# All engine orders of a fused attention and snake MLP kernel planned anew, with later assumed landings for units 4 to 11

## The chip, the core and the metric

One core of a Trainium2 chip. The metric is the time of one execution in microseconds on the device; lower is better.

## The reference

Two layers, one after the other, in float32 (the kernel works in bf16 with float32 sums):

```python
# linear attention with decay, blocks of 64 positions; B, H, S, D = 4, 8, 768, 64
for b in range(S // 64):
    qb, kb, vb = q[:, :, sl], k[:, :, sl], v[:, :, sl]
    intra = einsum('bhij,bhjd->bhid', einsum('bhic,bhjc->bhij', qb, kb) * Dmask, vb)
    inter = einsum('bhid,bhde->bhie', qb * lam_pow, kv_state)
    out[:, :, sl] = intra + inter
    kv_state = lam_block * kv_state + einsum('bhsd,bhse->bhde', kb * rev_pow, vb)
# snake MLP on x = out as 3072 tokens x 512
h = x @ w_in                     # 512 x 2048
g = h + sin(alpha * h) ** 2 / (alpha + 1e-9)
y = g @ w_out                    # 2048 x 512
```

## The kernel before

The attention is cut into 12 units (u = 0 to 11) of one batch and 256 positions, all eight heads. The MLP is cut into 6 chunks of 512 tokens; chunk c takes the outputs of units 2c and 2c+1.

For one unit the steps are:
- Loads of k, q and v (512 KB each) on SyncE's queue (`load_unit`, line 385 issues them), into one of three float32 buffers.
- Preparation, `uscale`: k is cast to bf16 (line 509), q and v are multiplied by powers of lam (line 523). There are two halves of heads of each, so six operations, each given to POOL, VectorE (DVE) or, for k, ScalarE (ACT). The result is `qkv`, a ring of three units.
- Transposes of q and k into `qkT`. Units 0 to 3 do it on TensorE (`upiece_T`, line 539, with a copy in line 548); units 4 to 11 do it by two DMA transposes on SyncE's queue (`upiece_D`, line 555).
- Matmuls in small tiles (line 578): scores, state sums and outputs (`urun` for the first units, `upair` for units 4 to 11, where one piece holds the scores and sums of unit u with the outputs of unit u-1). VectorE masks the scores (`Smu`, lines 658 and 767) and keeps the states (`Zs`, lines 671 and 778); ScalarE or POOL casts the states (`Zu`, lines 674 and 781); the outputs go to `xT` (lines 688 and 788).

For a chunk, an "a" unit is h for 128 of the 2048 columns and all 512 tokens (`unit_A`, four matmuls, line 811); an "h" unit is 256 columns and half of the tokens (`unit_A2`, eight matmuls, line 845). ScalarE takes the sine (t, lines 821 and 855), POOL or ScalarE the square (u, lines 825, 826, 859 and 860), VectorE joins them (gT, lines 828 and 863). A "b" unit is four of the 16 matmuls that give one 128 x 512 tile of the result (`unit_B`, line 876); after the fourth, ScalarE copies it out (line 890) and stores it.

The order of the work is set by a planner that runs when the kernel is built (`_Plan`). Every operation is given with an assumed duration; a DMA also with an assumed latency `lat` behind its transfer. The planner starts, one after the other, the operation that can begin first by these assumptions. SyncE keeps the order in which the program gives its operations (for each unit u: its transposes, then the loads of unit u+2). TensorE may take any of its next 40. ScalarE, VectorE and POOL take whatever is ready by the assumed times. Nothing of this is decided at run time: each engine then executes its fixed order, and waits at an operation whose inputs are not there.

Two lists written out by hand steer it. `HEAD` gives the loads and steps of units 0 and 1, with an engine and a bank behind the colon: `lk01` loads half 1 of unit 0's k, `q00:POOL` prepares half 0 of unit 0's q on POOL, `Tq01:2ACT` transposes by bank 2 with the copy on ACT, `S`, `O` and `Z` are scores, outputs and sums, `W` casts a staged part of w_in, `D` and `E` are loads of w_in and w_out in POOL's queue, with the load that they wait for behind the colon, and `F` is the order of free PSUM banks. `ORDER` is TensorE's list from there on: `a`, `h` and `b` units (chunk, then numbers), `g` for the next attention piece (18 in all; the tenth begins unit 4, the eleventh unit 5, and so on) and `s`, which leaves out one PSUM bank in the rotation of free banks. Matmuls of constants (`spin`, line 947) fill TensorE's idle time in the first 26 us of the plan.

Of the kernel before, what the change touches and what calls it, by code (L numbers as in the profile page):

```python
# [35 lines left out]
class _Plan:  # L36
# [21 lines left out]
    def op(self, eng, emit, dur, reads=(), writes=(), dma=None, after=(), issue=0.4, lat=2.6, runs=64):  # L58
        o = _Op(eng, emit, dur, tuple(reads), tuple(writes), dma, after, issue, lat, runs)
        for b in o.reads:  # L60
            if b in self.writer:
                o.deps.add(self.writer[b])
        for b in o.writes:
            if b in self.writer:
                o.deps.add(self.writer[b])
            o.deps.update(self.readers.get(b, ()))
        o.deps.update(after)
        for b in o.reads:
            self.readers.setdefault(b, []).append(o)
        for b in o.writes:  # L70
            self.writer[b] = o
            self.readers[b] = []
        o.deps.discard(o)
        o.lead = self.lead
        self.ops.append(o)
        return o
# [211 lines left out]
def bass_lightning_attn__then__act_snake_kernel(  # L288
# [34 lines left out]
    with es:  # L323

        def sb(name, shape, dt):
            return es.enter_context(nc.sbuf_tensor(name, shape, dt))
# [19 lines left out]
        qkT = sb("qkT", [128, RT, 8, 128], BF16)  # L346
# [25 lines left out]
        def _(_unused_eng):  # L372
# [4 lines left out]
            op = P.op  # L377
# [6 lines left out]
            def load(dst, src, key, dur, sem, eng="SP", lat=2.6, after=(), issue=0.4, runs=64):  # L384
                return op(eng, lambda e: e.dma_start(dst, src), dur, dma=sem, lat=lat, after=after, issue=issue, runs=runs,  # L385
                          writes=key if isinstance(key, list) else [key])

            def at(u):

                return 2 * (u // NB) + u % 2, u % NB // 2  # L390

            def load_unit(u, which, g=None, after=()):
                (b, n), j = at(u), u % (RL // 2)
                for nm in which:
                    src = {"q": q, "k": k, "v": v}[nm]
                    hs = slice(0, H) if g is None else slice(4 * g, 4 * g + 4)
                    if nm == "q":
                        dst = q32[j][:, hs, :, :].rearrange("p h t d -> p h (t d)")
                        keys = [("q32", j, i) for i in range(2) if g in (None, i)]
                    else:  # L400
                        dst = (k32 if nm == "k" else v32)[j][:, :].rearrange("p (h x) -> p h x", x=2 * D)[:, hs, :]
                        keys = [(nm + "32", 2 * j + i) for i in range(2) if g in (None, i)]
                    last[nm, u] = last[nm, u, g] = load(
                        dst, src[b, hs, 2 * BL * n:2 * BL * (n + 1), :].rearrange("h (p t) d -> p h (t d)", t=2),
                        keys, 1.82 if g is None else 0.91, f"u{nm}{j}" + ("" if g is None else str(g)),
                        lat=2.7 if g is None else 2.9, after=after, runs=64 if g is None else 32,
                    )

            def load_w1(i, after):
# [17 lines left out]
            def load_w2(i, after):  # L427
# [6 lines left out]
            last = {}  # L434
            load(lam_bc[:, :], bass.AP(lam.tensor, 0, [[0, 128], [1, H]]), "lam", 0.1, "lam", "ACT", runs=1)
            load(alphaT[:, :], bass.AP(moe_alpha.tensor, 0, [[128, NM], [1, 128]]), "alphaT", 0.1, "alphaT", "ACT", lat=4.9, runs=1)
            HEAD = """lk01 lv00 lq00 lk00 lv01 F:1564073 lq01 lq10 q00:POOL lk10 q01:POOL lk11 k11:ACT lq11 Tq01:2ACT lv10
                lv11 k10:POOL Tq00:1ACT q10:POOL v01:DVE k01:POOL D1:v11 k00:POOL Tk00:0ACT lw256 q11:DVE Tk01:7DVE
                S0:0 Tk1:2ACT lw0 D2:w0 v00:DVE Z0:6 S1:0 X0 O0:5 v10:POOL v11:POOL W256:ACT Z1:4 Tq1:0ACT O1:6 X1
                S2:6 S3:0 D3:v11 O3:0 E0:q11 W0:DVE A0.2:7 E1:w0 O2:4 A0.0:6""".split()  # L440
            for item in HEAD:
                if item[0] == "l":
                    if item[1] == "w":
                        load_w1_first(int(item[2:]))
                    else:
                        load_unit(int(item[2]), item[1], int(item[3]))
# [47 lines left out]
            def reg_keys(u, which, g):  # L494
                return [("u" + which, u % 3, g)]
# [5 lines left out]
            def uT_key(u, which, g):  # L501
                return ("qT" if g == 0 else "kT", 2 * (u % 3) + (which == "k"))
# [49 lines left out]
            def upiece_D(u, which):  # L552
                sl, i = 2 * (u % 3) + (which == "k"), 0 if which == "q" else 1024
                flat = qkv[:, 2 * (u % 3):2 * (u % 3) + 2, :, :].rearrange("p a b c -> p (a b c)")[:, i:i + 1024]
                op("SP", lambda e: e.dma_start_transpose(qkT[:, sl, :, :], flat), 1.0,  # L555
                   [x for g in range(2) for x in reg_keys(u, which, g)], [uT_key(u, which, g) for g in range(2)],
                   dma=f"qkT{sl}", runs=16, lat=2.1, issue=1.3)

            made = {}

# [308 lines left out]
            def unit_B(c, s4, mq, ob, lo=0, hi=DM, out_eng="ACT"):  # L869
# [26 lines left out]
                    return store  # L896
                store(out_eng)

            ORDER = """h0.1.2 h0.1.0 h0.1.12 h0.1.4 b0.0.0 h0.1.6 b0.2.0 h0.0.14 h0.0.4 a0.9 h0.0.12 g b0.1.0 h0.1.14
                h0.0.6 a0.8 s s b0.1.1 s s a0.10 g a0.11 s g s b0.2.1 b0.0.1 b0.1.2 b0.2.2 g b0.1.3 g b0.0.2 s  # L900
                b0.0.3 s s s g g g g h1.0.6 h1.0.0 b0.3.0 s b0.3.1 b0.2.3 h1.0.12 a1.9 s b0.3.2 s s b0.3.3 g a1.2
                a1.3 h1.1.6 a1.8 h1.1.0 a1.4 b1.0.0 a1.5 a1.11 a1.10 a1.14 a1.15 b1.0.1 h1.1.12 s b1.0.2 g s b1.0.3
                g b1.1.0 b1.1.1 b1.2.0 h2.0.4 b1.1.2 h2.0.10 a2.0 a2.7 b1.2.1 a2.1 a2.2 a2.6 s b1.1.3 b1.2.2 h2.1.4
                b1.3.0 b1.2.3 s a2.3 s g s s s b1.3.1 h2.1.10 b1.3.2 b1.3.3 s h2.0.14 h2.0.12 b2.0.0 a2.8 a2.9
                b2.1.0 s h2.1.14 h3.0.8 s s b2.0.1 h3.0.4 s b2.1.1 s b2.1.2 b2.0.2 s s s s b2.0.3 s g h2.1.12 s s
                a3.7 h3.0.0 h3.1.0 s s b2.2.0 b2.2.1 b2.1.3 b2.3.0 a3.14 h3.0.2 a3.6 h3.1.4 b2.2.2 a3.15 b2.3.1
                b2.2.3 s g s b2.3.2 s a3.12 s b2.3.3 s b3.0.0 b3.1.0 s h3.0.10 a3.13 h3.1.2 s b3.0.1 s s s s b3.0.2
                b3.0.3 b3.1.1 s s h3.1.8 s b3.1.2 g s a4.8 s h3.1.10 b3.1.3 b3.3.0 s b3.2.0 a4.1 s b3.2.1 a4.6
                b3.2.2 b3.2.3 s g s a4.2 a4.9 b3.3.1 a4.3 a4.0 s s b3.3.2 g s s b4.1.0 a4.5 a4.15 a4.10 a5.4 s s s
                a4.7 b3.3.3 s a4.13 a4.4 s b4.3.0 s b4.0.0 s a5.6 s s s s s a5.3 a5.12 a5.11 b4.3.1 b4.0.1 b4.2.0  # L910
                a5.8 s a4.11 a5.7 a5.13 s b4.1.1 a5.9 b4.1.2 s s a5.15 s a5.0 a5.2 b4.0.2 a5.5 a5.1 b4.2.1 a4.14 s
                a4.12 b5.2.0 s b4.2.2 a5.10 s s s b5.3.0 s b4.3.2 b4.0.3 b5.1.0 s s b5.3.1 b5.1.1 s a5.14 b5.1.2
                b5.0.0 b5.1.3 s b4.2.3 b5.0.1 b5.0.2 b5.0.3 b5.2.1 b4.3.3 b4.1.3 b5.3.2 b5.2.2 s b5.2.3 b5.3.3"""
            late = {}
            for item in HEAD:
                name, _, what = item.partition(":")
                kind = name[0]
                u, g = int(name[1]) if name[1:2].isdigit() else None, int(name[-1]) if name[-1].isdigit() else None
                if kind in "kqv":
                    uscale(u, kind, g, what)  # L920
                elif kind == "T":
                    u, gs = int(name[2]), [int(x) for x in name[3:]] or [0, 1]
# [35 lines left out]
            for u in range(2, U0):  # L958
                s = 2 * u
# [11 lines left out]
            for u in range(U0, NU + 1):  # L971
                if u < UD:
                    pieces += [([4], lambda u=u: upiece_T(u, "k", [0, 1], 4)), ([5], lambda u=u: upiece_T(u, "q", [0, 1], 5))]
                pieces.append(([1, 2, 3, 4, 5, 6, 7], lambda u=u: upair(
                    u if u < NU else None, u - 1 if u > U0 else None)))
                outs_at[u - 1] = len(pieces) if u > U0 else outs_at[u - 1]
            ahead = [(0, lambda: load_unit(2, "kqv", None, [last["w1", 3]])), (0, lambda: load_w2(3, [last["k", 2]])),
                     (0, lambda: load_unit(3, "kqv"))]
            for u in range(2, NU):
                ahead.append((outs_at[u - 3] if u > 4 else 0, lambda u=u: uprep(u)))  # L980
                for which in "kq" if u >= UD else "":
                    ahead.append((0, lambda u=u, which=which: upiece_D(u, which)))
                if u + 2 < NU:
                    ahead.append((0, lambda u=u: load_unit(u + 2, "kqv")))
            done, todo = 0, ORDER.split()
            for i, token in enumerate(todo):
# [71 lines left out]
```

## Time and profile before

| what | value |
| --- | --- |
| median of 3 runs | 219.35 us (218.84 to 219.45) |
| the profiled execution | 219.23 us, span 217.5 us |
| granted TensorE clock | 1.00 |
| TensorE, matmuls | 202.1 us busy, 93% of the span |
| ScalarE | 145.0 us busy, 67% |
| VectorE | 130.8 us busy, 60% |
| POOL | 98.3 us busy, 45% |
| moved by DMA | 34.45 MB |

Busy time counts an engine's instructions; "idle before" and the bracket at the end of a timeline row give the engine's idle time just before an instruction and what ended it. PE is TensorE, SPq is SyncE's DMA queue. A row of stretches holds the length, then for each engine the busy time and in brackets the instructions, then granted clock, DMA share and GB/s. A row of waits holds the sum in us, the number of waits and the longest.

### The profile page before, as it was taken

The numbers are of one execution on the slowest core, as the hardware profiler recorded it, in microseconds if no ns is written. First come the engines' busy times: TensorE is split into PE (matmuls) and PEld (weight loads), VectorE is DVE, ScalarE is ACT, GpSimd is POOL, SyncE is SP. The second block draws the span as 40 slices with busy tenths as digits, with TensorE's granted clock in tenths as the row PEclk, the third lists the DMA queues.
The fourth block names the chain that finished last, engine by engine and source line by source line (L and its number), as shares of the span: only waits on it lengthen the run. The fifth ranks groups of instructions, "written<-read, shape, count | busy, mean of one in ns | idle before, by whom it ended". The sixth has DMA issues, their size and how long they took to land.

```text
span 217.5 us, 5371 instructions
## 1 busy us (share of the span) xinstructions
PE 202.1 (93%) x2251; PEld 113.3 (52%) x2274; DVE 130.8 (60%) x214; ACT 145.0 (67%) x263; POOL 98.3 (45%) x110
## 2 busy tenths in 40 slices
PE   4899999799989897999699999999999999999995
PEld 1355775364645455555465655556454444444454
DVE  2676668788889964754683674844457555652100
ACT  2586789453769735786585885864869688794431
POOL 2577768364577965751972751510006231310000
PEclk9999999999999999999999999999999999999999
DMA  4999999999999999999993911502011000001242
GB/s 111 300 311 227 207 267 268 242 276 323 274 236 271 292 214 301 228 222 285 189 294 102 127 24 56 92 2 99 3 48 51 0 0 0 3 2 62 79 150 99
DMA packets 62985, 34.45 MB, mean 158 GB/s; under 512 B 18272, under 2 KB 60016, under 8 KB 62960
## 3 DMA queue, kind: packets, MB, share of 16 engines
q1 hardware_dynamic: 55632, 24.25, 50.0%
q0 software_dynamic: 3696, 3.67, 10.2%
q10 hardware_dynamic: 3632, 6.17, 8.3%
q8 instruction: 18, 0.29, 0.6%
q14 instruction: 7, 0.06, 0.1%
HBM read 27.28 MB, written 6.29 MB: 154 GB/s over the span
## 4 chain that ended last, share of the span: by engine, by line
PE 57%; DMA 22%; POOL 6%; SPq 5%; DVE 4%; issue 2%; ACT 2%; ACTq 0%
PE bank L876 28%; PE bank L811 16%; DMA q<-in_q_dram 9%; PE bank L845 7%; DMA v<-in_v_dram 6%; PE bank L578 6%; DMA w<-in_moe_w_in_dram 4%; SPq L385 4%; POOL qkv L523 3%; DMA k<-in_k_dram 2%; POOL u L826 2%; DVE Smu L767 1%; SPq L555 1%; DVE gT L828 1%; DVE qkv L523 1%
## 5 line engine op out<-in xcount | busy, mean ns | idle before, releaser
L876 PE MATMUL bank<-w,gT 128*128 128x512 bf16 (+1 forms) x383 | 88.0, 370 | 3.1 <-issue 1.4
L828 DVE SCALAR_TENSOR_TENSOR gT<-u,rinv,bank 128x512 bf16<-128x512 bf16 x60 | 43.5, 744 | 27.1 <-ACT u L825 17.0
L876 PEld LDWEIGHTS bank<-w,gT 128*128 128x128 bf16 x400 | 38.0, 98 | 41.5 <-DVE gT L828 1.7
L811 PE MATMUL bank<-xT,w 128*128 128x512 bf16 x234 | 56.1, 379 | 0.5 <-issue 0.2
L821 ACT ACTIVATE t<-bank,alpha 128x512 bf16<-128x512 f32 x60 | 39.9, 686 | 13.1 <-PE bank L811 12.2
L863 DVE SCALAR_TENSOR_TENSOR gT<-u,rinv,bank 128x256 bf16<-128x256 bf16 x72 | 31.2, 475 | 13.6 <-POOL u L860 9.8
L845 PE MATMUL bank<-xT,w 128*128 128x256 bf16 x288 | 35.5, 273 | 1.9 <-DVE Smu L767 1.8
L811 PEld LDWEIGHTS bank<-xT,w 128*128 128x128 bf16 x240 | 22.9, 98 | 27.1 <-ACT xT L788 1.1
L855 ACT ACTIVATE t<-bank,alpha 128x256 bf16<-128x256 f32 x72 | 30.4, 472 | 9.7 <-PE bank L845 9.1
L845 PEld LDWEIGHTS bank<-xT,w 128*128 128x128 bf16 x288 | 27.5, 98 | 10.1 <-DVE Smu L767 2.7
L826 POOL TENSOR_TENSOR u<-t 128x512 bf16<-128x512 bf16 x21 | 21.7, 1039 | 22.5 <-ACT t L821 15.1
L860 POOL TENSOR_TENSOR u<-t 128x512 bf16<-128x512 bf16 x23 | 24.0, 1057 | 11.4 <-ACT t L855 11.4
L890 ACT COPY osb<-bank 128x512 f32<-128x512 f32 (+1 forms) x25 | 14.2, 568 | 18.9 <-PE bank L876 18.9
L767 DVE TENSOR_TENSOR Smu<-bank,masku 128x1024 bf16<-128x1024 f32 x16 | 19.0, 1219 | 11.0 <-PE bank L578 11.0
L825 ACT ACTIVATE u<-t 128x512 bf16<-128x512 bf16 x39 | 24.4, 629 | 1.0
L523 POOL TENSOR_TENSOR qkv<-q,Lq 128x512 bf16<-128x512 f32 x15 | 17.5, 1177 | 15.9 <-DMA q<-in_q_dram 15.9
L523 POOL TENSOR_TENSOR qkv<-v,Lv 128x512 bf16<-128x512 f32 x16 | 18.0, 1134 | 13.2 <-PE bank L578 9.3
L788 ACT CAST xT<-bank 128x512 bf16<-128x512 f32 x15 | 10.5, 741 | 7.6 <-PE bank L578 7.6
L947 PE MATMUL bank<-masku,ident 128*128 128x512 bf16 x33 | 10.8, 435 | 2.7 <-DVE masku L461 2.7
L523 DVE TENSOR_TENSOR qkv<-q,Lq 128x512 bf16<-128x512 f32 x9 | 7.4, 821 | 7.4 <-DMA q<-in_q_dram 7.4
L509 POOL CAST qkv<-k 128x512 bf16<-128x512 f32 x12 | 7.3, 611 | 8.5 <-DMA k<-in_k_dram 8.5
L658 DVE TENSOR_TENSOR Smu<-bank,masku 128x1024 bf16<-128x1024 f32 x8 | 9.7, 1218 | 2.2 <-PE bank L578 2.2
(56 smaller groups left out, 139.8 us busy)
## 6 DMA issues: line engine op xcount, KB each, us to landing
out_dram<-osb ACTq DMA_DIRECT2D x23, 256.0 KB, 2.4
k<-in_k_dram SPq DMA_DIRECT2D x10, 512.0 KB, 5.4
q<-in_q_dram SPq DMA_DIRECT2D x10, 512.0 KB, 7.2
v<-in_v_dram SPq DMA_DIRECT2D x10, 512.0 KB, 8.0
w<-in_moe_w_out_dram POOLq DMA_DIRECT2D x4, 512.0 KB, 8.7
w<-in_moe_w_in_dram POOLq DMA_DIRECT2D x3, 512.0 KB, 9.3
k<-in_k_dram SPq DMA_DIRECT2D x4, 256.0 KB, 5.5
v<-in_v_dram SPq DMA_DIRECT2D x4, 256.0 KB, 5.3
```

Of the source, the lines that this page charges most:

```text
L523: emit = lambda e: e.tensor_tensor(dst, src, tab, ALU.mult)
L767: op("DVE", lambda e, g=g: e.tensor_tensor(Smu[(2 * S + g) % 4][:, :, :, :, :].rearrange("p a b c i -> p (a b) (c i)"), bass.AP(banks, 512 ...
L811: ins = e.matmul(ps[hb][:, c0:c1], w1[:, kc, 128 * m:128 * (m + 1)], xT[x][:, kc, c0:c1], start=(kc == 0 and c0 == lo), stop=(kc == NKC - ...
L821: op("ACT", lambda e: e.activation(t16[ju][:, w], ps[hb][:, w], ACTF.Sin, scale=alpha[:, m:m + 1]), 0.69 * f, [bank(hb), "alpha"], [("t16" ...
L825: lambda e: (e.activation(u16[ju][:, w], t16[ju][:, w], ACTF.Square) if e is nc.scalar else e.tensor_tensor(u16[ju][:, w], t16[ju][:, w], ...
L826: e.tensor_tensor(u16[ju][:, w], t16[ju][:, w], t16[ju][:, w], ALU.mult)), 0,
L828: op("DVE", lambda e: e.scalar_tensor_tensor(out=gT[g][:, m, w], in0=u16[ju][:, w], scalar=rinv[:, m:m + 1], in1=ps[hb][:, w], op0=ALU.mul ...
L845: ins = e.matmul(ps[hb][:, 256 * i:256 * i + 256], w1[:, kc, 128 * (m + i):128 * (m + i + 1)], xT[x][:, kc, lo:lo + 256], start=(kc == 0 a ...
L855: op("ACT", lambda e, i=i: e.activation(t16[ju][:, 256 * i:256 * i + 256], ps[hb][:, 256 * i:256 * i + 256], ACTF.Sin, scale=alpha[:, m + ...
L860: e.tensor_tensor(u16[ju][:, :], t16[ju][:, :], t16[ju][:, :], ALU.mult)), 0,
L863: op("DVE", lambda e, i=i: e.scalar_tensor_tensor(out=gT[g][:, m + i, lo:lo + 256], in0=u16[ju][:, 256 * i:256 * i + 256], scalar=rinv[:, ...
L876: ins = e.matmul(ps[ob][:, w], gT[g][:, m, 128 * s4:128 * (s4 + 1)], w2[:, m, w], start=(m == 0), stop=(m == NM - 1),)
```

## The change

Three assumed numbers are raised: the latency of the loads of units 4 to 11 from 2.7 to 5.0, and the transfer and the latency of a DMA transpose from 1.0 to 1.45 and from 2.1 to 2.5. `HEAD` and `ORDER` are replaced. The planner makes all the engines' orders from these, so the order of every engine can differ. The loads, the transposes and the arithmetic stay the same, except that two column pairs more are done as h units and fewer as a units (60 a and 36 h before, 56 a and 40 h after, with the two `A` steps of `HEAD` counted as h). The b units are the same in another order, and `ORDER` has 210 `s` instead of 89.

How many a, h and b units stand ahead of a piece in `ORDER`:

| piece | g10 | g11 | g12 | g13 | g14 | g15 | g16 | g17 | g18 |
| --- | --- | --- | --- | --- | --- | --- | --- | --- | --- |
| before | 34 | 49 | 50 | 68 | 86 | 102 | 116 | 126 | 132 |
| after | 38 | 52 | 52 | 65 | 85 | 97 | 114 | 130 | 132 |

```diff
--- before.py
+++ after.py
@@ -403,7 +403,7 @@
                     last[nm, u] = last[nm, u, g] = load(
                         dst, src[b, hs, 2 * BL * n:2 * BL * (n + 1), :].rearrange("h (p t) d -> p h (t d)", t=2),
                         keys, 1.82 if g is None else 0.91, f"u{nm}{j}" + ("" if g is None else str(g)),
-                        lat=2.7 if g is None else 2.9, after=after, runs=64 if g is None else 32,
+                        lat=(2.7 if u < 4 else 5.0) if g is None else 2.9, after=after, runs=64 if g is None else 32,
                     )
 
             def load_w1(i, after):
@@ -434,10 +434,10 @@
             last = {}
             load(lam_bc[:, :], bass.AP(lam.tensor, 0, [[0, 128], [1, H]]), "lam", 0.1, "lam", "ACT", runs=1)
             load(alphaT[:, :], bass.AP(moe_alpha.tensor, 0, [[128, NM], [1, 128]]), "alphaT", 0.1, "alphaT", "ACT", lat=4.9, runs=1)
-            HEAD = """lk01 lv00 lq00 lk00 lv01 F:1564073 lq01 lq10 q00:POOL lk10 q01:POOL lk11 k11:ACT lq11 Tq01:2ACT lv10
-                lv11 k10:POOL Tq00:1ACT q10:POOL v01:DVE k01:POOL D1:v11 k00:POOL Tk00:0ACT lw256 q11:DVE Tk01:7DVE
-                S0:0 Tk1:2ACT lw0 D2:w0 v00:DVE Z0:6 S1:0 X0 O0:5 v10:POOL v11:POOL W256:ACT Z1:4 Tq1:0ACT O1:6 X1
-                S2:6 S3:0 D3:v11 O3:0 E0:q11 W0:DVE A0.2:7 E1:w0 O2:4 A0.0:6""".split()
+            HEAD = """lk00 lv00 lq00 lk01 k01:POOL lv01 lq01 v01:POOL q00:POOL lk10 k00:DVE Tk00:7ACT lq10 lk11 Tq00:6DVE
+                lq11 k10:ACT q01:POOL lv11 lv10 F:5164073 q10:DVE q11:DVE v00:DVE Tk01:2DVE Z0:6 S0:1 v10:POOL
+                D1:q11 X0 Tq01:2DVE lw256 k11:ACT Tk1:1DVE O0:4 v11:DVE S1:4 Tq1:2ACT S2:0 Z1:4 D2:w256 lw0 X1 S3:1
+                O2:4 D3:v11 W0:ACT W256:ACT O3:1 E0:q11 O1:6 A0.2:7 E1:w256 A0.0:6""".split()
             for item in HEAD:
                 if item[0] == "l":
                     if item[1] == "w":
@@ -552,9 +552,9 @@
             def upiece_D(u, which):
                 sl, i = 2 * (u % 3) + (which == "k"), 0 if which == "q" else 1024
                 flat = qkv[:, 2 * (u % 3):2 * (u % 3) + 2, :, :].rearrange("p a b c -> p (a b c)")[:, i:i + 1024]
-                op("SP", lambda e: e.dma_start_transpose(qkT[:, sl, :, :], flat), 1.0,
+                op("SP", lambda e: e.dma_start_transpose(qkT[:, sl, :, :], flat), 1.45,
                    [x for g in range(2) for x in reg_keys(u, which, g)], [uT_key(u, which, g) for g in range(2)],
-                   dma=f"qkT{sl}", runs=16, lat=2.1, issue=1.3)
+                   dma=f"qkT{sl}", runs=16, lat=2.5, issue=1.3)
 
             made = {}
 
@@ -896,21 +896,24 @@
                     return store
                 store(out_eng)
 
-            ORDER = """h0.1.2 h0.1.0 h0.1.12 h0.1.4 b0.0.0 h0.1.6 b0.2.0 h0.0.14 h0.0.4 a0.9 h0.0.12 g b0.1.0 h0.1.14
-                h0.0.6 a0.8 s s b0.1.1 s s a0.10 g a0.11 s g s b0.2.1 b0.0.1 b0.1.2 b0.2.2 g b0.1.3 g b0.0.2 s
-                b0.0.3 s s s g g g g h1.0.6 h1.0.0 b0.3.0 s b0.3.1 b0.2.3 h1.0.12 a1.9 s b0.3.2 s s b0.3.3 g a1.2
-                a1.3 h1.1.6 a1.8 h1.1.0 a1.4 b1.0.0 a1.5 a1.11 a1.10 a1.14 a1.15 b1.0.1 h1.1.12 s b1.0.2 g s b1.0.3
-                g b1.1.0 b1.1.1 b1.2.0 h2.0.4 b1.1.2 h2.0.10 a2.0 a2.7 b1.2.1 a2.1 a2.2 a2.6 s b1.1.3 b1.2.2 h2.1.4
-                b1.3.0 b1.2.3 s a2.3 s g s s s b1.3.1 h2.1.10 b1.3.2 b1.3.3 s h2.0.14 h2.0.12 b2.0.0 a2.8 a2.9
-                b2.1.0 s h2.1.14 h3.0.8 s s b2.0.1 h3.0.4 s b2.1.1 s b2.1.2 b2.0.2 s s s s b2.0.3 s g h2.1.12 s s
-                a3.7 h3.0.0 h3.1.0 s s b2.2.0 b2.2.1 b2.1.3 b2.3.0 a3.14 h3.0.2 a3.6 h3.1.4 b2.2.2 a3.15 b2.3.1
-                b2.2.3 s g s b2.3.2 s a3.12 s b2.3.3 s b3.0.0 b3.1.0 s h3.0.10 a3.13 h3.1.2 s b3.0.1 s s s s b3.0.2
-                b3.0.3 b3.1.1 s s h3.1.8 s b3.1.2 g s a4.8 s h3.1.10 b3.1.3 b3.3.0 s b3.2.0 a4.1 s b3.2.1 a4.6
-                b3.2.2 b3.2.3 s g s a4.2 a4.9 b3.3.1 a4.3 a4.0 s s b3.3.2 g s s b4.1.0 a4.5 a4.15 a4.10 a5.4 s s s
-                a4.7 b3.3.3 s a4.13 a4.4 s b4.3.0 s b4.0.0 s a5.6 s s s s s a5.3 a5.12 a5.11 b4.3.1 b4.0.1 b4.2.0
-                a5.8 s a4.11 a5.7 a5.13 s b4.1.1 a5.9 b4.1.2 s s a5.15 s a5.0 a5.2 b4.0.2 a5.5 a5.1 b4.2.1 a4.14 s
-                a4.12 b5.2.0 s b4.2.2 a5.10 s s s b5.3.0 s b4.3.2 b4.0.3 b5.1.0 s s b5.3.1 b5.1.1 s a5.14 b5.1.2
-                b5.0.0 b5.1.3 s b4.2.3 b5.0.1 b5.0.2 b5.0.3 b5.2.1 b4.3.3 b4.1.3 b5.3.2 b5.2.2 s b5.2.3 b5.3.3"""
+            ORDER = """h0.1.6 h0.1.0 b0.0.0 h0.1.2 h0.0.6 a0.4 b0.2.0 a0.5 h0.1.14 h0.1.8 s s s h0.0.14 s s g a0.13 b0.1.0
+                s s s h0.0.8 a0.11 g a0.10 b0.1.1 s s a0.12 b0.0.1 s s b0.1.2 g s b0.1.3 s s s g g s s s b0.0.2 s s
+                s s b0.3.0 s b0.0.3 s s s b0.2.1 s s b0.3.1 s s b0.2.2 g s g s s s s b0.2.3 s s h1.0.6 g g h1.0.12 s
+                b0.3.2 a1.0 a1.9 s s a1.8 a1.3 h1.0.4 s s a1.10 s b0.3.3 s s s g a1.1 h1.1.4 a1.2 a1.11 b1.0.0
+                h1.1.14 h1.1.6 b1.0.1 s h1.0.14 s h1.1.12 b1.1.0 b1.1.1 s b1.0.2 s b1.0.3 s s s g g s s b1.1.2 s s s
+                s a2.4 b1.1.3 b1.3.0 b1.3.1 s s a2.5 s s s s h2.0.2 h2.1.2 s b1.2.0 a2.1 s s s s s s s b1.2.1 b1.3.2
+                s b1.3.3 g s h2.0.6 h2.1.6 a2.0 h2.1.10 b1.2.2 s a2.8 b1.2.3 s s s s b2.0.0 a2.9 s a2.14 s b2.1.0
+                b2.1.1 s h2.0.10 b2.0.1 s s s h2.0.12 h3.0.8 s a2.15 s h3.0.4 b2.0.2 s b2.0.3 s g s s b2.2.0 h2.1.12
+                b2.1.2 h3.0.2 a3.0 s s s s b2.1.3 b2.2.1 s s a3.1 b2.3.0 s s h3.1.4 s b2.2.2 b2.2.3 g s h3.1.14
+                h3.0.10 s s b2.3.1 h3.1.6 s s s s h3.0.6 h3.0.12 s h3.1.12 s b2.3.2 h3.0.14 s b3.0.0 s h3.1.8 s s s
+                s b3.0.1 b2.3.3 s s s s s b3.0.2 b3.0.3 h3.1.2 b3.1.0 s g a4.1 h3.1.10 b3.1.1 s a4.6 s s b3.1.2 a4.8
+                s s a4.3 s a4.4 b3.2.0 s b3.2.1 s b3.1.3 s b3.3.0 s a4.13 s b3.2.2 b3.2.3 b3.3.1 s s g a4.15 b3.3.2
+                s g s s s a4.2 a4.0 s s s s s a4.9 s a4.7 s s a4.5 a5.11 b4.1.0 s s b3.3.3 b4.3.0 s s s s s s a5.12
+                s a4.10 s a5.4 b4.1.1 a5.7 s s b4.2.0 s a5.5 a5.15 s s s a4.11 b4.0.0 a5.1 b4.0.1 s a5.2 a5.3 s a5.9
+                s s s a4.14 b4.2.1 a5.0 s s b5.1.0 a5.6 s s b4.2.2 a5.10 s s s s b4.3.1 b5.1.1 a5.8 b5.1.2 s s a5.14
+                s a4.12 s b4.0.2 s s a5.13 s s s s s s s s b5.0.0 b4.0.3 s b4.3.2 b5.3.0 s s b4.3.3 b5.3.1 b5.2.0 s
+                s s b5.0.1 s s b4.1.2 b5.3.2 s s s s b5.2.1 s b4.1.3 s b5.0.2 s s s b4.2.3 s b5.3.3 b5.2.2 b5.0.3
+                b5.1.3 b5.2.3 s"""
             late = {}
             for item in HEAD:
                 name, _, what = item.partition(":")
```

## The prediction

> **What bounds the kernel now.** I read the page's first two parts first, then the table of stretches, then TensorE's own waits, and last the timeline around each wait.
>
> ```profile
> span 217.5 us, 5371 instructions
> ...
> PE 202.1 (93%) x2251; PEld 113.3 (52%) x2274; DVE 130.8 (60%) x214; ACT 145.0 (67%) x263; POOL 98.3 (45%) x110
> ...
> PEclk9999999999999999999999999999999999999999
> DMA  4999999999999999999993911502011000001242
> ```
>
> TensorE (PE) is busy 93% of the span at full granted clock; no other engine is near. The transfers are dense for 21 slices (to about 114 us) and sparse after. So the end is: start of the unbroken matmul run, plus the matmuls, plus PE's idle time on the way. The table by stretch says where that idle time lies.
>
> ```profile
> 21.70:36.00 14.30, 14.20 (x110) 10.58 (x111) 10.28 (x23) 12.10 (x28) 10.43 (x11) 1.00 1.22 237
> 36.00:60.00 24.00, 22.11 (x340) 12.78 (x343) 20.07 (x31) 14.26 (x25) 13.00 (x15) 1.00 1.10 283
> 60.00:80.00 20.00, 18.17 (x226) 10.05 (x228) 16.51 (x28) 14.94 (x29) 16.43 (x17) 1.00 1.19 248
> 80.00:110.00 30.00, 26.36 (x344) 15.18 (x346) 18.27 (x29) 19.13 (x39) 17.67 (x17) 1.00 1.17 250
> 110.00:160.00 50.00, 49.36 (x651) 29.66 (x657) 28.59 (x52) 34.88 (x64) 16.46 (x20) 1.00 0.39 84
> 160.00:214.90 54.90, 54.33 (x307) 26.22 (x312) 24.30 (x33) 36.88 (x59) 11.71 (x12) 1.00 0.11 42
> ```
>
> Length, then PE's busy time: idle is 0.10, 1.89, 1.83, 3.64, 0.64 and 0.57 us. From 60 to 110 us, where the preparation of units 5 to 10 mixes with chunk 1 and 2 of the second layer pair, it is 5.47; in the 105 us behind it, 1.21. Nothing can be won after 110 us. PE's waits, by what ended them:
>
> ```profile
> PE bank L845 <- DVE Smu L767: 1.8, 1, 1.8
> ...
> PE bank L578 <- ACT Zu L781: 1.4, 1, 1.4
> PE bank L578 <- DVE Zs L778: 0.9, 1, 0.9
> ...
> PE bank L876 <- DVE gT L828: 0.6, 1, 0.6
> ```
>
> Four single waits (Smu, Zu, Zs, gT L828) make 4.67 of the 5.47 us. The timeline says what stood before each releaser on its own engine:
>
> ```profile
> 82.69 0.62 ACT L509 CAST qkv<-k 128x512 bf16<-128x512 f32 x1 [2.56 <-DMA k<-in_k_dram]
> 83.21 0.40 ACT L781 CAST Zu<-Zs 128x256 bf16<-128x256 f32 x1
> 83.67 0.42 PE L578 MATMUL bank<-Smu,qkv 64*64 64x128 bf16 x16 [1.35 <-ACT Zu L781]
> ...
> 80.96 0.41 DVE L778 TENSOR_TENSOR Zs<-Zs,bank 128x256 f32<-128x256 f32 x1
> ...
> 103.50 0.69 DVE L523 TENSOR_TENSOR qkv<-q,Lq 128x512 bf16<-128x512 f32 x1 [2.96 <-DMA q<-in_q_dram]
> 104.11 2.35 DVE L767 TENSOR_TENSOR Smu<-bank,masku 128x1024 bf16<-128x1024 f32 x2
> ...
> 101.28 0.22 PE L578 MATMUL bank<-qkT 64*64 64x128 bf16 x2
> ...
> 105.39 3.05 PE L845 MATMUL bank<-xT,w 128*128 128x256 bf16 x24 [1.83 <-DVE Smu L767]
> ```
>
> At 83.67 us ScalarE stood 2.56 us in front of unit 8's k, which had not landed, with Zu, which PE needed, behind it; its input Zs was ready at 81.37. At 105.39 VectorE stood 2.96 us in front of unit 10's q, with Smu behind it, though the scores were out at 101.50. These two, 3.18 us, are just what the change speaks of: preparation placed ahead of its landing.
>
> **The change part by part.**
>
> *Later assumed landings (2.7 to 5.0 for loads of units 4 to 11; transposes 1.0 to 1.45 and 2.1 to 2.5).* These numbers issue nothing; they act through the order. Zu without the cast in front: 81.37 + 0.40 = 81.8, before PE came free at 83.67 - 1.35 = 82.32, so the whole 1.35 goes if unit 6's transposes have landed. Smu without the q product in front: 101.50 plus half of 2.35 is 102.7, before 103.56, so the whole 1.83 goes. The other two, with two rows of the chain of waits that price a matmul piece (3.45 / 4 = 0.86 us of full width, 1.75 / 2 = 0.87 of half width):
>
> ```profile
> 63.27 0.72 PE L578 MATMUL bank<-qkT 64*64 64x128 bf16 x32 [0.87 <-DVE Zs L778]
> ...
> 70.61 1.04 POOL L523 TENSOR_TENSOR qkv<-v,Lv 128x512 bf16<-128x512 f32 x1
> 71.61 3.11 POOL L826 TENSOR_TENSOR u<-t 128x512 bf16<-128x512 bf16 x3
> ...
> 76.23 1.04 PE L876 MATMUL bank<-w,gT 128*128 128x512 bf16 x4 [0.62 <-DVE gT L828]
> ...
> 114.51 3.45 PE bank L876 x16
> ...
> 123.04 1.75 PE bank L845 x16
> ```
>
> Unit 4's score matmuls (63.27) stood in PE's order ahead of the landing of their transposes: the second was issued at 57.7 and took 5.4 us, which is 63.1 (rows below). In the new list this piece (the tenth g) stands behind 38 matmul pieces instead of 34, 4 x 0.86 = 3.4 us later: 0.87 goes. The 0.62 at 76.23 hangs on products (u) that POOL had behind unit 6's preparation: it goes if that moves. Upper end of the gain: 1.35 + 1.83 + 0.87 + 0.62 = 4.67 us.
>
> *What is late next.* SyncE issues in the order of the program: transposes of unit u, then loads of unit u+2. So later preparation delays both. The rows for the transposes of units 4, 5, 6, 7 and 8 (first and last start, then time to landing; each pair from one answer):
>
> ```profile
> L555 SPq DMA_TRANSPOSE qkT<-qkv x2: 1935/2867/3799, 53.8 to 57.7; - x2
> DMA to landing us min/median/max: 5.4/6.9/8.5
> ...
> L555 SPq DMA_TRANSPOSE qkT<-qkv x2: 2991/3180/3370, 71.2 to 74.7; - x2
> DMA to landing us min/median/max: 5.0/6.3/7.5
> ...
> L555 SPq DMA_TRANSPOSE qkT<-qkv x2: 1383/3188/4992, 89.8 to 94.9; - x2
> DMA to landing us min/median/max: 3.4/5.5/7.6
> ```
>
> (Shown are 4, 6 and 8.) Unit 6: 74.7 + 5.0 = 79.7, used at 83.67: 4.0 us of slack. Unit 8: 94.9 + 3.4 = 98.3; its scores run in the piece that begins at 117.9, 19.6 us later. The delay that the change assumes is at most 2.3 + 0.4 + 2 x 0.45 = 3.6 us a unit, and the chain from load to transposes to load runs over every second unit: 3.6 for units 4 and 5, 7.2 for 6 and 7, 10.8 for 8. Unit 8's slack covers that; unit 6's falls short by at most 3.2 us. The cover there is stock: behind the twelfth g the new list holds 10 more chunk 1 pieces of 0.86 us, 8.6 us that need nothing of unit 6. So I cost it at nothing; without that cover it costs 3.2.
>
> *New waits from a new order.* No row prices an order that has not run. Lower end 0. Upper end by the nearest stretch, 36 to 60 us, which has the same engines loaded and no wait of the four kinds: 1.89 idle in 24 us, 0.079 a us, which over 60 to 106 makes 3.6; 0.8 of it is there already (5.47 - 4.67), so 2.8. I take 2.0, nearer to the upper end, since that is what this planner leaves on this chip when VectorE is over 80% busy.
>
> *The head made anew.* Same loads but for the order of halves. POOL gives up three of its eight preparations, VectorE has five instead of three; of six copies of transposes ScalarE keeps two (before five); the cast W0 goes from VectorE to ScalarE. What this sets is the start of the unbroken run:
>
> ```profile
> 16.77 1.05 ACT L424 CAST w<-ws 128x1024 bf16<-128x1024 f32 x1 [0.42 <-DMA ws<-in_moe_w_in_dram]
> ...
> 19.67 0.74 POOL L385 DMA_DIRECT2D w<-in_moe_w_in_dram  x1 [1.27 <-DMA ws<-in_moe_w_in_dram]
> ...
> 20.62 0.68 DVE L424 CAST w<-ws 128x1024 bf16<-128x1024 f32 x1
> ...
> 21.73 4.57 PE L845 MATMUL bank<-xT,w 128*128 128x256 bf16 x40
> ```
>
> The second staged weight slice landed by 19.67 and was cast at 20.62, 0.95 late. A free ScalarE could begin 0.95 earlier and take 0.37 longer (1.05 against 0.68): -0.6 at best. At worst the cast waits behind one more operation of about 1.2 us there (two Smu take 2.35) and takes its 0.37: +1.5. I take 0: the landing, which the edit hardly moves, is the larger part. The POOL's weight loads come about 2 to 3 us earlier in its queue (two gates name an earlier landing), but the one that gates unit 2's loads remains third, so those stay near their 26.9 us.
>
> VectorE and POOL side by side are dearer than either alone:
>
> ```profile
> 95.08 0.69 DVE L523 TENSOR_TENSOR qkv<-q,Lq 128x512 bf16<-128x512 f32 x1 [1.33 <-DMA q<-in_q_dram]
> 95.12 1.55 POOL L523 TENSOR_TENSOR qkv<-q,Lq 128x512 bf16<-128x512 f32 x1 [3.80 <-DMA q<-in_q_dram]
> ```
>
> POOL's product took 1.55 beside VectorE's, against 1.04 alone at 70.61. The Trainium skill (Perfetto Trace Analysis, Optimizing Scalar/DVE Operations) says that the two share a read port, so that moving work between them may not help; the two rows agree, and by it one more such pair in the head would make the sum 0.5 us longer.
>
> *Tail and forms.* Four full-width units become half-width ones, which cost PE 0.01 us more each by the two rows of the chain: nothing. The last pieces of the list again put matmuls between the last outputs: nothing.
>
> **Sum.** -4.67 + 2.0 + 0 = -2.67. The profiled execution took 219.23 us (span 217.5 and 1.73 around it), 0.12 below the median of 219.35; 219.35 - 2.67 = 216.7.
>
> **The rivals.**
>
> *Slower: the SyncE chain eats unit 6's slack.* Place: the twelfth g. If real preparation is later by over 4.0 us and PE's order does not let the 8.6 us of stock go first, PE waits up to 3.2 us there, and the other three waits are replaced by like ones: 219.35 + 3.2 - 1.35 = 221.2. For it: SyncE already issues unit by unit about 9 us apart (71.2 for unit 6, 89.8 for unit 8). Against: slack and stock above. It decides from about 3.3 us of such wait on (2.67 of gain and 0.66 to be seen). 0.20.
>
> *No change.* The waits come back elsewhere in the new order (2.8) and the head costs the rest, 1.5: -4.67 + 2.8 + 1.5 = -0.4, 219.0. For it: VectorE at over 80% from 36 to 80 us, whatever the order. 0.15.
>
> *The whole gain.* No new wait and a better head: -4.67 - 0.6 gives 214.1. Against it speaks the 36 to 60 stretch. 0.07.
>
> *The clock drops.* A wait of PE of some 4 us in the twelfth g, followed by a slow clock: 3.4 us of matmuls at half speed would add 1.7 to the first rival, 222.9. PE's longest wait behind the start is 1.83, and the granted clock is 1.00 in every stretch, so no row shows it: 0.03. The Trainium skill (TensorE: Matmul & The Clock Gate, What's actually happening) states that an idle window of about 3.4 us halves the clock; no run here shows that.
>
> **How the numbers follow.** The forecast has 0.55, with 215.0 to 218.6 as its own range. Under 0.3% (0.66 us) the runs cannot be told from no change, so faster is 0.55 + 0.07 = 0.62, same 0.15, slower 0.20 + 0.03 = 0.23. The range reaches from 214.8 (between the forecast and the whole gain) to 221.0 (most of the first rival).
>
> **What would show it.** Right: from 60 to 110 us PE's idle time falls from 5.5 to about 2.8; no wait of PE on Zu or Smu behind a cast or product that waits for a DMA; those preparation rows show shorter DMA waits on ScalarE and VectorE; the unbroken run starts within 1 us of 21.7. Wrong: PE waits of over 1 us on qkT landings near the eleventh to thirteenth g; transposes further apart than 9 us a unit with work missing; or a run that starts later than 23 us.

## The result

The changed kernel takes 216.33 us (median of 4 runs, 216.08 to 216.58) against 219.4 us: ratio 0.9856, 95% interval 0.9821 to 0.9892. Measured again beside other kernels it is 216.11 us against 219.68, ratio 0.9840 (0.9806 to 0.9875). The forecast was 216.7. The medians here and below leave out the executions that took over 1.5% longer than the fastest of their kernel: one of the kernel before, two of kernel 1 in the table below (one of them 1188 us) and one of kernel 3. The profiled execution took 216.58 us, its span 2.7 us less than before. Its page:

```profile
span 214.8 us, 5435 instructions
...
PE 205.0 (95%) x2290; PEld 114.9 (53%) x2290; DVE 136.6 (64%) x225; ACT 143.5 (67%) x264; POOL 93.9 (44%) x106
...
PEclk9999999999999999999999999999999999999999
```

By stretch (length, then PE's busy time):

```profile
20.00:36.00 16.00, 14.95 (x145) 10.01 (x142) 11.34 (x23) 12.77 (x27) 7.66 (x8) 1.00 1.21 238
36.00:60.00 24.00, 23.93 (x350) 13.60 (x349) 19.46 (x31) 15.04 (x28) 13.96 (x14) 1.00 1.09 281
60.00:80.00 20.00, 18.66 (x185) 10.58 (x186) 17.04 (x29) 15.74 (x31) 13.95 (x15) 1.00 1.21 239
80.00:110.00 30.00, 29.06 (x433) 17.53 (x422) 23.56 (x37) 21.83 (x44) 20.31 (x21) 1.00 1.15 246
110.00:160.00 50.00, 50.00 (x666) 30.41 (x664) 30.38 (x54) 33.80 (x66) 19.69 (x22) 1.00 0.40 90
```

PE's idle time from 60 to 110 us is 1.34 + 0.94 = 2.28 us; it was 5.47, and "about 2.8" was forecast. What PE still waits for behind the start of the unbroken run, by releaser:

```profile
PE bank L876 <- ACT osb L890: 0.7, 1, 0.7
PE bank L539 <- ACT qkv L509: 0.5, 1, 0.5
PE bank L811 <- DVE gT L828: 0.5, 1, 0.5
...
PE bank L578 <- DVE gT L863: 0.4, 1, 0.4
PE bank L876 <- DVE gT L863: 0.4, 1, 0.4
...
PE bank L578 <- DVE gT L828: 0.2, 1, 0.2
PE bank L845 <- DVE gT L828: 0.2, 1, 0.2
```

No wait on Zu, Smu or Zs is left. In the timeline the releasers now stand ahead of the preparation on their engines:

```profile
83.19 0.41 DVE L778 TENSOR_TENSOR Zs<-Zs,bank 128x256 f32<-128x256 f32 x1
83.64 0.40 ACT L781 CAST Zu<-Zs 128x256 bf16<-128x256 f32 x1 [0.41 <-DVE Zs L778]
83.95 0.61 ACT L509 CAST qkv<-k 128x512 bf16<-128x512 f32 x1
85.96 2.36 DVE L767 TENSOR_TENSOR Smu<-bank,masku 128x1024 bf16<-128x1024 f32 x2 [2.35 <-PE bank L578]
...
88.23 0.68 DVE L523 TENSOR_TENSOR qkv<-q,Lq 128x512 bf16<-128x512 f32 x1
...
96.48 0.69 DVE L523 TENSOR_TENSOR qkv<-q,Lq 128x512 bf16<-128x512 f32 x1 [0.62 <-DMA q<-in_q_dram]
97.59 1.23 DVE L767 TENSOR_TENSOR Smu<-bank,masku 128x1024 bf16<-128x1024 f32 x1 [0.42 <-PE bank L578]
...
99.75 1.21 DVE L767 TENSOR_TENSOR Smu<-bank,masku 128x1024 bf16<-128x1024 f32 x1
...
107.79 1.10 DVE L523 TENSOR_TENSOR qkv<-q,Lq 128x512 bf16<-128x512 f32 x1
```

Zu comes first, then unit 8's k, which waits for no transfer; both Smu of unit 6 (85.96) come ahead of unit 8's q, and both of unit 7 (97.59 and 99.75) ahead of unit 10's q (107.79). One product still waits 0.62 us for its landing ahead of a Smu (unit 9's q, 96.48); that Smu then waited for PE in any case, so it cost nothing.

### The profile page after: what moved, and what is told of

It reads as the page before. It is cut to its first block, busy times and chain, and to the rows that moved or that the text cites. A ratio compares the mean times of both kernels' runs of the same rounds, so it can differ in the third digit from the quotient of the medians.

```text
span 214.8 us, 5435 instructions
## 1 busy us (share of the span) xinstructions
PE 205.0 (95%) x2290; PEld 114.9 (53%) x2290; DVE 136.6 (64%) x225; ACT 143.5 (67%) x264; POOL 93.9 (44%) x106
## 4 chain that ended last, share of the span: by engine, by line
PE 78%; DMA 11%; POOL 3%; SPq 3%; ACT 2%; issue 1%; DVE 0%; POOLq 0%
PE bank L876 38%; PE bank L811 18%; PE bank L845 13%; PE bank L578 7%; DMA w<-in_moe_w_in_dram 5%; DMA k<-in_k_dram 3%; SPq L385 3%; DMA q<-in_q_dram 3%; POOL u L826 2%; PE bank L539 1%; POOL w L385 1%; ACT t L821 1%; POOL qkv L523 1%; ACT osb L890 0%; DVE gT L828 0%
## 5 line engine op out<-in xcount | busy, mean ns | idle before, releaser
L828 DVE SCALAR_TENSOR_TENSOR gT<-u,rinv,bank 128x512 bf16<-128x512 bf16 x56 | 40.7, 744 | 22.0 <-ACT u L825 13.4
L811 PE MATMUL bank<-xT,w 128*128 128x512 bf16 x224 | 53.1, 379 | 0.8 <-DVE gT L828 0.5
L821 ACT ACTIVATE t<-bank,alpha 128x512 bf16<-128x512 f32 x56 | 37.4, 685 | 12.2 <-PE bank L811 11.4
L863 DVE SCALAR_TENSOR_TENSOR gT<-u,rinv,bank 128x256 bf16<-128x256 bf16 x80 | 34.3, 475 | 12.8 <-POOL u L860 7.3
L845 PE MATMUL bank<-xT,w 128*128 128x256 bf16 x320 | 38.7, 273 | 0.2 <-DVE gT L828 0.2
L855 ACT ACTIVATE t<-bank,alpha 128x256 bf16<-128x256 f32 x80 | 32.9, 474 | 6.6 <-PE bank L845 5.0
L811 PEld LDWEIGHTS bank<-xT,w 128*128 128x128 bf16 x224 | 21.5, 98 | 25.7 <-DVE gT L828 1.0
L845 PEld LDWEIGHTS bank<-xT,w 128*128 128x128 bf16 x320 | 30.5, 98 | 8.2 <-ACT xT L788 1.5
L523 POOL TENSOR_TENSOR qkv<-q,Lq 128x512 bf16<-128x512 f32 x13 | 15.0, 1159 | 11.5 <-DMA q<-in_q_dram 11.5
L509 ACT CAST qkv<-k 128x512 bf16<-128x512 f32 x11 | 6.8, 617 | 6.0 <-DMA k<-in_k_dram 6.0
L578 PE MATMUL bank<-qkT,Zu 64*64 64x128 bf16 x160 | 10.3, 221 | 0.3
```

What stands on the lines that cost most here:

```text
L523: emit = lambda e: e.tensor_tensor(dst, src, tab, ALU.mult)
L578: ins = e.matmul(to, w, x, start=(b, c) not in seen, stop=True, skip_group_check=True)
L811: ins = e.matmul(ps[hb][:, c0:c1], w1[:, kc, 128 * m:128 * (m + 1)], xT[x][:, kc, c0:c1], start=(kc == 0 and c0 == lo), stop=(kc == NKC - ...
L821: op("ACT", lambda e: e.activation(t16[ju][:, w], ps[hb][:, w], ACTF.Sin, scale=alpha[:, m:m + 1]), 0.69 * f, [bank(hb), "alpha"], [("t16" ...
L828: op("DVE", lambda e: e.scalar_tensor_tensor(out=gT[g][:, m, w], in0=u16[ju][:, w], scalar=rinv[:, m:m + 1], in1=ps[hb][:, w], op0=ALU.mul ...
L845: ins = e.matmul(ps[hb][:, 256 * i:256 * i + 256], w1[:, kc, 128 * (m + i):128 * (m + i + 1)], xT[x][:, kc, lo:lo + 256], start=(kc == 0 a ...
```

## The experiments

The theory: PE's waits come from preparation that stands ahead of its landing, and go when it stands later. The rival: any new set of orders moves them about; what counts is how well one whole plan fits.

**Two places of the old orders, nothing else.**

```diff
 ScalarE:  +Zu (unit 5)              VectorE:  +Smu x2 (unit 7)
            k, half 0 (unit 8)                  q, half 1 (unit 10)
           -Zu (unit 5)                        -Smu x2 (unit 7)
```

> The kernel before with two places of its engine orders changed and nothing else: on ScalarE the cast of half 0 of unit 8's k stands behind Zu of unit 5 instead of ahead of it, and on VectorE the product of half 1 of unit 10's q stands behind the two Smu of unit 7 instead of ahead of them. Landing theory: PE's waits of 1.35 us (on Zu) and 1.83 us (on Smu) go, 219.4 - 3.2 = 216.2 us, with all other waits as before. Rival (the waits only move): PE waits again within the next piece, 218.7 us or more.

Measured 218.66 us, ratio 0.9933 (0.9907 to 0.9959): by the medians (219.72 beside it) 1.06 us, a third of the 3.18, by the interval 0.9 to 2.0. That is close to the rival's number. Both waits are gone, and one came back (line numbers are 19 to 21 higher here; L798 is Zs, L786 Smu, L542 the products):

```profile
81.35 0.40 ACT L801 CAST Zu<-Zs 128x256 bf16<-128x256 f32 x1 [1.27 <-DVE Zs L798]
...
87.65 0.69 DVE L542 TENSOR_TENSOR qkv<-v,Lv 128x512 bf16<-128x512 f32 x1 [1.34 <-DMA v<-in_v_dram]
...
88.25 1.22 DVE L786 TENSOR_TENSOR Smu<-bank,masku 128x1024 bf16<-128x1024 f32 x1
...
90.32 1.90 PE L897 MATMUL bank<-w,gT 128*128 128x512 bf16 x8 [1.58 <-DVE Zs L798]
```

PE came to that piece 1.5 us earlier (82.19 against 83.67); unit 8's v landed 1.3 us later than before (at about 87.6 against 86.3; why is not shown), and the product stood ahead of Smu and Zs.

**Two more such places.** Unit 8's q and v products behind one Smu each, too.

> The two-moves kernel with two more on VectorE: the products of half 1 of unit 8's q and v each stand behind one Smu of unit 6 instead of ahead of it (in the two-moves kernel they waited for their landings, and PE then waited 1.58 us at 90.32 and 0.41 later). Theory that the wait comes back because the next preparation also stands ahead of its landing: 218.6 - 1.6 = 217.0 us, 216.5 to 217.4. Rival (the stretch is bound by the amount of work on VectorE and POOL): 218.6 us within 0.5.

Measured 219.04 us, ratio 0.9952 (0.9920 to 0.9984): no better than two moves. The 1.58 us shrank to 0.38, but unit 9 was next: VectorE waited for its k, then ran gT and unit 9's q (1.54 us), with the gT that PE needed behind them:

```profile
93.83 0.43 DVE L528 CAST qkv<-k 128x512 bf16<-128x512 f32 x1 [1.29 <-DMA k<-in_k_dram]
...
95.68 1.54 DVE L542 TENSOR_TENSOR qkv<-q,Lq 128x512 bf16<-128x512 f32 x1
...
97.93 1.04 PE L832 MATMUL bank<-xT,w 128*128 128x512 bf16 x4 [1.05 <-DVE gT L849]
```

So one wait can be taken out by its place, but PE then runs on to the next operation that stands behind a landing. The number is the rival's; that the wait comes back behind the next preparation is what the theory said.

**The numbers alone** (old `HEAD` and `ORDER`):

```diff
-lat=2.7 if g is None else 2.9
+lat=(2.7 if u < 4 else 5.0) if g is None else 2.9
 # and, for the transposes, 1.0 to 1.45 and lat=2.1 to lat=2.5
```

> The kernel before with the three raised numbers and its old HEAD and ORDER. Landing theory: the numbers alone put the preparation behind Zu and Smu; the waits of 1.35 and 1.83 us are gone and some new ones of up to 1.5 us come: 217.0 us, between 216.2 and 218.0. Rival (the two new lists carry the gain, the numbers only helped to find them): 219.4 us within 0.7.

Measured 219.71 us, ratio 1.0005 (0.9972 to 1.0039): the rival's number. The old waits on Zu and on the later Smu are gone, and others came, two of them between 60 and 80 us, where VectorE was busy for 18.08 of the 20 us. None of the three rows has a landing on VectorE or ScalarE ahead of its releaser:

```profile
66.62 1.05 PE L845 MATMUL bank<-xT,w 128*128 128x256 bf16 x8 [1.52 <-DVE Smu L767]
...
78.79 1.76 PE L876 MATMUL bank<-w,gT 128*128 128x512 bf16 x4 [1.74 <-DVE gT L828]
...
84.55 1.90 PE L876 MATMUL bank<-w,gT 128*128 128x512 bf16 x8 [0.68 <-ACT osb L890]
```

**The lists alone** (new `HEAD` and `ORDER`, the old numbers):

> The changed kernel with the old numbers (2.7; 1.0 and 2.1). Landing theory: preparation stands ahead of its landing again, and PE has waits of 1 us and more behind it between 60 and 110 us: 218.5 us or more. Rival (the new lists carry the gain): 216.5 us within 0.7.

Measured 223.1 us, ratio 1.0143 (1.0110 to 1.0176): slower, as the landing theory said. Unit 6's q and v stand ahead of their landings on VectorE, and gT behind them:

```profile
67.53 0.69 DVE L523 TENSOR_TENSOR qkv<-q,Lq 128x512 bf16<-128x512 f32 x1 [0.52 <-DMA q<-in_q_dram]
...
68.14 0.74 DVE L828 SCALAR_TENSOR_TENSOR gT<-u,rinv,bank 128x512 bf16<-128x512 bf16 x1
...
68.94 1.18 PE L578 MATMUL bank<-qkT 64*64 64x128 bf16 x32 [1.44 <-DVE gT L828]
...
69.28 1.39 DVE L523 TENSOR_TENSOR qkv<-v,Lv 128x512 bf16<-128x512 f32 x1 [0.39 <-DMA v<-in_v_dram]
...
71.39 3.59 PE L845 MATMUL bank<-xT,w 128*128 128x256 bf16 x16 [1.27 <-DVE gT L828]
```

VectorE's waits for the landings (0.52 and 0.39) are shorter than PE's behind them (1.44 and 1.27), so they are a part of the loss only; another part is PE's clock (last section).

**One list or one number taken back.** All others as in the changed kernel.

```diff
 1: HEAD as before     2: ORDER as before
 3: transposes 1.0 and 2.1 again, loads 5.0
 4: loads 2.7 again, transposes 1.45 and 2.5
 5: loads 3.5          6: loads 7.0
```

> The changed kernel with the old HEAD (new ORDER and new numbers). If the new HEAD only moved the start of the unbroken run (22.08 us against 21.73 before), this is 0.35 us shorter: 216.0 us. Rival (the new ORDER fits only its own HEAD): new waits between 22 and 60 us, 217.3 us or more.

> The changed kernel with the old ORDER (new HEAD, new numbers). If HEAD and the numbers carry part of the gain by themselves: 218.0 us or less. If the lists fit only together: 219.5 us or more, with PE waits of over 1 us between 60 and 110 us.

> The changed kernel with the old numbers for the transposes (1.0 and 2.1) and the raised one for the loads (5.0). If the assumed landing of the loads is what keeps the preparation behind: 216.5 us within 0.7. Rival (the lists fit one plan only, and any change of a number spoils it): 218 us or more.

> The changed kernel with the old number for the loads (2.7) and the raised ones for the transposes. If the loads' number is what counts, preparation stands ahead of its landing as with all old numbers: waits of 1 us and more at 66 to 72 us, 220 us or more. Rival (the transposes' numbers, which keep the attention pieces behind, count): 217 us or less.

> The changed kernel with 3.5 instead of 5.0 for the loads of units 4 to 11. If the time follows the assumed landing: between lists-only (223.1 at 2.7 with old transposes; 219.3 with the new ones) and 216.2, so about 218. If the lists fit only the plan that they were found with: 218.5 to 222, on no line with the number.

> The changed kernel with 7.0 instead of 5.0 for the loads of units 4 to 11. If later is better or harmless (units 7 to 11 have 10 us and more of slack): 216.5 us within 0.7. If the lists fit only the plan that they were found with: 218.5 to 222.

| taken back | us | ratio to before, 95% interval |
| --- | --- | --- |
| 1 HEAD | 220.64 | 1.0050 (1.0013 to 1.0087) |
| 2 ORDER | 222.67 | 1.0132 (1.0092 to 1.0172) |
| 3 transposes' numbers | 220.98 | 1.0054 (1.0014 to 1.0095) |
| 4 loads' number | 219.28 | 0.9967 (0.9939 to 0.9995) |
| 5 loads 3.5 | 220.77 | 1.0057 (1.0033 to 1.0081) |
| 6 loads 7.0 | 219.01 | 0.9975 (0.9949 to 1.0002) |

All six are 2.7 to 6.3 us slower than the changed kernel. Kernels 2, 3, 5 and 6 came out as the second half of their expectation said, that the lists fit one plan only. Kernel 1 did by its number, but its two longest waits lie at 70.4 and 94.2 us and not between 22 and 60; kernel 4 missed both halves (its waits at 66 to 72 us are 0.90 and 0.83 us). The time does not follow the number: 2.7, 3.5, 5.0 and 7.0 with the same lists give 219.3, 220.8, 216.1 and 219.0. Raising the loads' number further, to 7.0, loses the gain too. PE's clock has a part in it (last section): in kernel 6 it fell in nine of ten executions, and the tenth took 217.45 us.

The waits that come are elsewhere in each. The longest of kernel 6 and of kernel 2 are on gT, with no landing ahead of it on VectorE:

```profile
68.78 0.64 PE L578 MATMUL bank<-qkv 64*64 64x64 bf16 x16 [2.45 <-DVE gT L863]
```

```profile
80.27 0.42 PE L578 MATMUL bank<-Smu,qkv 64*64 64x128 bf16 x16 [2.54 <-DVE gT L828]
```

In kernel 3 one is on the copy osb, and the next is of the landing kind again: ScalarE stood 1.86 us in front of unit 10's k, with the output xT that PE needed behind it.

```profile
84.65 1.04 PE L876 MATMUL bank<-w,gT 128*128 128x512 bf16 x4 [1.42 <-ACT osb L890]
...
101.95 0.62 ACT L509 CAST qkv<-k 128x512 bf16<-128x512 f32 x1 [1.86 <-DMA k<-in_k_dram]
...
102.47 0.72 ACT L788 CAST xT<-bank 128x512 bf16<-128x512 f32 x1
...
103.25 1.92 PE L845 MATMUL bank<-xT,w 128*128 128x256 bf16 x16 [1.19 <-ACT xT L788]
```

So is its longest: at 112.9 VectorE and POOL had waited 1.32 and 2.53 us for unit 11's q, and PE then waits 1.64 us at 118.07 for a gT behind it. Both theories have a part: preparation ahead of its landing comes back in some plans, and in the others PE waits as long without it.

**Waits of the changed kernel itself, moved.**

```diff
 VectorE: v, half 0 (unit 5) behind Smu x2 (unit 4)
 PE:      transposes of unit 2's k behind the next h unit; one b unit behind the next h unit
```

> The changed kernel itself, as the measure for the three beside it: 216.3 us, 0.986 of the kernel before.

> The changed kernel with three operations moved later in their engine's order and nothing else: VectorE's product of half 0 of unit 5's v stands behind the two Smu of unit 4 (it stood ahead of gT results for which PE then waits 0.52, 0.40, 0.22 and 0.20 us between 65 and 69 us), the transposes of unit 2's k stand one h unit later on PE (wait of 0.55 at 34.69), and one b unit one h unit later (wait of 0.36 at 31.38). Theory that each wait ends with what stands ahead of its releaser: up to 2.25 us go; with a third of it staying as in the two-moves kernel (1.06 of 3.18), between 0.75 and 2.25: 215.0 us, 214.1 to 215.6. Rival (the waits are set by the amount of work on VectorE and POOL in this stretch and come back a little later): 216.3 us within 0.4.

Measured 216.2 us against 216.11 of the changed kernel beside it: nothing, as the rival said. The waits that were moved turn up a little later (line numbers are 19 to 27 higher):

```profile
64.74 1.04 POOL L542 TENSOR_TENSOR qkv<-v,Lv 128x512 bf16<-128x512 f32 x1
...
66.04 0.87 DVE L888 SCALAR_TENSOR_TENSOR gT<-u,rinv,bank 128x256 bf16<-128x256 bf16 x2 [0.42 <-ACT u L884]
...
66.97 0.44 PE L598 MATMUL bank<-qkv 64*64 64x64 bf16 x16 [0.58 <-DVE gT L888]
```

```profile
36.23 1.04 PE L902 MATMUL bank<-w,gT 128*128 128x512 bf16 x4 [0.79 <-DVE qkT L568]
```

VectorE stood idle for 0.42 us before 66.04 and waited for ScalarE's u: with the product out of the way another engine's work set the time. That speaks for the rival in this stretch. No version that was run beats the changed kernel.

## Why the prediction was right, point by point

- *What bounds it.* Right: the span fell by 2.7 us. PE's waits of over 0.3 us behind its start were 0.53, 0.74, 0.87, 0.62, 1.35 and 1.83, in all 5.94; now 0.36, 0.55, 0.52, 0.40, 0.68 and two of 0.2, in all 2.93. With the run starting 0.35 later that is 2.66. This accounts for the profiled pair (216.58 against 219.23); the medians fell by 3.1 and 3.6 us, and a part of the rest is the clock of the kernel before (last section).
- *The four waits, -4.67.* All gone, as forecast.
- *New waits, +2.0.* Between 60 and 110 us they are 0.52 + 0.40 + 0.22 + 0.20 + 0.68 = 2.02. The size was right by luck: the rate behind it was not a property of the stretch, since 36 to 60 us, from which it was taken, itself fell from 1.89 idle to 0.07. There two waits (1.27) left, and two new ones before 36 us (0.91) and the later start (0.35) took 1.26 back. None of these three was in the sum, and that they cancelled is luck too.
- *The head, 0 (-0.6 to +1.5).* The run starts at 22.08 instead of 21.73: +0.35, inside the range.
- *"These numbers act through the order".* This was the weak step. It let the two direct waits, 3.18 us, follow from the later landings alone. The numbers alone gave nothing, and the two places alone 1.06 us. The whole gain was measured only for both lists and all three numbers together; what makes just this plan fit stays open.
- *What is late next.* The transposes of units 4, 5, 6 and 7 were issued at these times (SyncE's timeline, start first), within 0.8 us of before (53.75, 62.73, 71.25 and 80.80):

```profile
54.05 5.51 SPq L555 DMA_TRANSPOSE qkT<-qkv  x2
...
63.51 5.39 SPq L555 DMA_TRANSPOSE qkT<-qkv  x2
...
71.48 6.47 SPq L555 DMA_TRANSPOSE qkT<-qkv  x2
...
80.72 4.05 SPq L555 DMA_TRANSPOSE qkT<-qkv  x1
```

  Up to unit 7 the transposes hardly came later, although single preparations did, behind their neighbours in the order (unit 8's q on VectorE at 88.23 against 84.52). Unit 6's slack was not touched, and the slower rival did not come about. The later units' transposes did move (102.4 against 99.2 for unit 9), where there was slack.
- *The clock drops.* It did not in the changed kernel. But the rows that this rival was priced by, 1.00 in every stretch, are of one execution: in later ones of the kernel before, with its old orders, the clock did fall (last section).
- *A misreading.* The 0.64 us of idle time from 110 to 160 us, and the nine waits put down to "issue" (1.4 us), are gone with 400 matmul records in line 876 instead of 383; 400 is what the weight loads counted before too. They fit missing records better than idle time. The 5.47 and 0.8 us held some of it.

## What to carry to other kernels

In a plan with fixed orders, look for an engine that waits for a transfer with another engine's releaser behind it; that is where later placement can pay. Do not count on the sum of such waits from moving single operations: here only 1.06 of 3.18 us was won by the medians, since PE then met the next landing. Assumed latencies and the lists searched with them belong together: after either is changed, search the other anew and measure.

## What the runs showed of the hardware

PE's clock fell although no wait was long. With the lists alone, the stretch around the three waits (0.89, 1.44 and 1.27 us) reads, PE's busy time second and the granted clock third from the end:

```profile
66.00:68.00 2.00, 0.61 (x17) 0.33 (x16) 1.48 (x4) 2.00 (x5) 0.42 (x1) 1.00 1.20 291
68.00:70.00 2.00, 1.06 (x32) 0.94 (x32) 1.61 (x3) 1.61 (x3) 2.00 (x2) 0.61 1.25 284
70.00:72.00 2.00, 0.73 (x8) 0.43 (x4) 2.00 (x4) 0.00 (x0) 1.57 (x2) 0.50 0.80 199
72.00:74.00 2.00, 2.00 (x11) 1.40 (x10) 2.00 (x2) 0.69 (x2) 0.00 (x0) 0.50 1.17 319
```

The clock halved at about 68.4 us, during the second of these waits, when PE had been busy for 0.61 of the 2.4 us since 66.0; it was full again at about 75.2. PE was busy for 4.8 of these 6.8 us, so an estimate of the cost is half of that, 2.4 us. With the numbers alone the clock halved at about 79.0, right behind the single wait of 1.74 us. The prediction's fourth rival asked for one wait of some 4 us; these shorter ones were enough, but not always: in the profiled executions of kernels 1 and 2 the clock stayed at 1.00 through waits of 2.57 and 2.54 us. The Trainium skill (TensorE: Matmul & The Clock Gate, What's actually happening) speaks of an idle window of about 3.4 us; here no single idle stretch was that long, and PE had been busy for 1.61 of the 3.4 us ahead of the fall.

Over a whole execution the mean granted clock is then 0.99 or less instead of 1.00. So it was in 28 of 88 executions of the kernel before that were measured beside the experiments (median 221.1 us, against 219.5 of the other 60), in 4 of 12 with the numbers alone, in all 6 with the lists alone, in 33 of 58 of kernels 1 to 6, and in none of the 10 of the changed kernel or of the 30 with moved operations. Most of the gain does not come from the clock: beside the 216.11 us, the kernel before took 219.43 in its executions at full clock, 3.3 us more.

POOL's product took 1.04 us in the kernel with moved waits (64.74, above), where VectorE's product no longer ran beside it, and 1.49 in the changed kernel, where one of 1.20 us began at 63.98:

```profile
64.60 1.49 POOL L523 TENSOR_TENSOR qkv<-v,Lv 128x512 bf16<-128x512 f32 x1
```

That agrees with the read port that the two share by the Trainium skill (Perfetto Trace Analysis, Optimizing Scalar/DVE Operations).
